# One more unit of seven products, squares on ScalarE and a new work order in a fused attention and FFN kernel

## The chip, the cores and the metric

The kernel runs on one core of one Trainium2 chip. The metric is the device time of one execution in microseconds (us). The time before is the median of three runs, 202.79 us (202.77 to 202.88).

## The reference

All tensors are bf16; there are 2048 tokens and a width of 640, 32 heads of 20, and an FFN width of 1728.

```python
xn = layernorm(x)                                  # per token, no weights
q, k, v = heads(xn @ wqkv)                         # wqkv: 640 x 1920
pq, pk = phi(q), phi(k)                            # phi(t) = (t + 1 if t > 0 else exp(t)) + 1e-6
kv = sum over tokens of pk^T v; z = sum of pk      # linear attention, no mask
s = ((pq @ kv) / (pq . z + 1e-6)) @ wo
g = silu(relu(xn @ w1) @ w2)                       # w1: 640 x 1728, w2: 1728 x 640
return x + s * g
```

## The kernel before

Tokens are cut into 16 tiles of 128, and four tiles make a chunk of 512. The width of 640 gives five pieces of 128 for the contraction.

**Stages.** In the head, tiles 0 to 3 are centred with a quick mean (`mean_act`, `centre`), transposed on TensorE (`transposes`), copied out of PSUM (`xcT_copy`) and multiplied with the key weights (`K_mm`); the missing scale 1/sigma is applied later, for keys in `K_exp` and `K_relu`, for FFN blocks in `scale_h`. Tiles 4 to 15 get their statistics (`bn` twice and `aggr`, or `LN_stats`), are normalised (`LN_norm`) and transposed by a DMA that `LN_norm` issues on SP's queue (`xnT_dma`, L703); tiles 0 to 3 get that normalised and transposed copy later too. The keys, query blocks (`Q_block`, 128 columns of q for one chunk) and FFN blocks (`H_block`, 128 columns of h for one chunk) follow, then the token sum of pk and x (`g` units, `G_last`), the denominators, the matrix that joins kv with wo, the second FFN product (`u` units) and the output product (`o` units).

**Units of seven.** Many products are done in pairs by a scheme of seven half-size products for eight (`unit`, `seven`): sums of weights (`h_S`, `q_S`, `m_S`, `k_S`) and sums of activations (`h_T`) are made on VectorE, each unit runs the steps s1, s5, s6, s2, s7, s3, s4 on TensorE over three PSUM banks, with evacuations on ScalarE and adds on VectorE between them. Units `a` and `p` are FFN and query blocks for chunks 0 and 1 (`jp` = 0), `b` and `q` those for chunks 2 and 3, `k` key tiles. Query block 4 and FFN block 12 have no partner of their own kind; for chunks 2 and 3 they form a unit together (`m_unit`, `m1`), for chunks 0 and 1 they are four plain blocks of five 512-column matmuls: block 12 of chunk 0 in the head (`HP`), `H112`, `Q04` and `Q14`.

**Order.** Each operation is recorded with what it reads and writes; `place` then plays the records through a table of estimated costs. TensorE and SP keep the order in which operations were recorded; ScalarE, VectorE and GpSimd do so up to `end_of_head`, and behind it may take any of the next 60 operations that is ready. The order of recording is written out by hand: the head as Python calls, everything behind it as words of `PROGRAM`, a few of which are `a0.s1` (step s1 of unit a0), `H14` (FFN block 4 of chunk 1), `n8` (statistics and norm of tile 8), `Ka8` (half of key tile 8), `y7` (pk of tile 7 added to the sum by a GpSimd DMA), `l0` and `l1` (the two pieces of the last output tile, cut at column `LC[1]`).

**The head's order on TensorE:** 32 small matmuls on constants, key products and transposes of tiles 0 to 3 as their loads come, FFN blocks 4, 5, 10, 11, 12 of chunk 0 (L804), key tiles 4 to 7 (L714), FFN blocks 10, 12, 4, 11, 5 of chunk 1, `Q14` (L766), then unit `a0` (L1203). **On SP's queue:** x 0, key weights in four loads, w1 pieces, x 4 to 7, w1 pieces, the transposes of tiles 4, 5, 6, 7, x 8-9, query weights, the transposes of tiles 0 to 3. x 1 to 3 are loaded from ScalarE's queue.

Of the kernel before, what the change touches and what calls it, by code (L numbers as in the profile page):

```python
# [95 lines left out]
class Sched:  # L96
# [44 lines left out]
    def _record(self, E, kind, fns, R, W, extra, sem=None):  # L141
# [5 lines left out]
        if kind == "dma":  # L147
# [12 lines left out]
            o.byt = 0.6 if o.turn else size / {"scr": 205e3}.get(names[0], {"scr": 240e3}.get(names[1], 310e3))  # L160
            lag = 0.5 if names[1] == "scr" else 0.8 if names[1] == "reg3" and names[0] == "reg6" else 0.0
            if o.turn and names[0] == "wv_sb":
                o.byt = 2.0
# [25 lines left out]
    def place(self):  # L189
# [16 lines left out]
        line = 2.0  # L206
        narrow = turned = False
# [4 lines left out]
        while left:  # L212
# [133 lines left out]
H110 H112 H14 H111 T0 H15 SQ SK xa Q14 a0.s1 a0.s5 Q04 a0.s6 p1.s5 p1.s1 n8 wa xb a0.s2 a0.s7 p1.s6 rb a0.s3 a0.s4 p1.s3 a1.s5 a1.s1 wb p1.s7 p1.s2 a1.s6 xc n9 SH1 p1.s4 a1.s2 Kb8 a1.s7 n12 n11 p0.s1 n10 n13 a1.s3 p0.s5 Ka8 p0.s6 n14 a1.s4 n15 y7 p0.s2 a2.s5 a2.s1 p0.s7 Ka12 a2.s6 Kb12 p0.s3 a2.s2 p0.s4 y8 a2.s3 a2.s7 hh0 hh1 T1 a2.s4 b0.s1 b0.s5 Ka11 b0.s6 k1.s1 k1.s5 b0.s2 k1.s6 b0.s7 b0.s3 k1.s7 k1.s2 b0.s4 k1.s3 k1.s4 Kb15 q0.s1 q0.s5 b1.s1 q0.s6 b1.s5 q0.s2 b1.s6 q0.s7 y6 q0.s3 b1.s3 q0.s4 mv6 b1.s7 b1.s2 y2 k2.s5 k2.s1 b1.s4 a3.s5 y3 k2.s6 Kb11 y9 a3.s1 k2.s2 k2.s7 k2.s3 a3.s6 k2.s4 a3.s2 a3.s7 a3.s3 q1.s1 q1.s5 a3.s4 q1.s6 b2.s5 q1.s2 SM y12 b2.s1 y13 Ka15 y0 q1.s7 w2a b2.s6 y4 y1 y14 GT1 GT2 y5 y15 q1.s3 y11 q1.s4 b2.s7 zm b2.s3 GS0 GT3 b2.s2 b3.s1 b2.s4 b3.s5 SH2 y10 b3.s6 m1.s5 m1.s1 b3.s2 b3.s7 m1.s6 b3.s3 m1.s2 b3.s4 m1.s7 zs b4.s5 GT4 m1.s3 b4.s1 m1.s4 c1 b4.s6 b5.s5 b5.s1 w2d c0 b4.s7 b4.s2 b4.s3 b5.s6 b4.s4 g0.s5 w2b g0.s1 b5.s7 b5.s3 b5.s2 zc g0.s6 b5.s4 dn g0.s3 g1.s1 GS1 g1.s5 g1.s6 g0.s7 g0.s2 w2c g1.s7 g1.s3 wv0 ZS uT3 wo do0 g1.s2 g1.s4 g0.s4 wv1 sl rc0 uSa0 uSb0 uT2 uT1 do3 do1 u0.s1 u0.s5 kv1 u0.s6 rc1 kv0 W5 u0.s7 u0.s2 W4 uT4 uSa2 dv1 u0.s3 W2 u0.s4 W1 W3 W0 xre dv0 uSa1 u1.s1 oT uSb2 uSb1 u1.s5 u2.s1 u2.s5 u1.s6 u2.s6 u2.s2 uSa4 u2.s7 oS0 u1.s7 u1.s3 u2.s3 u1.s2 u2.s4 u1.s4 do2 o0.s5 o0.s1 u4.s5 o0.s6 u4.s1 o0.s2 o0.s3 uSb4 o0.s7 u4.s6 o0.s4 u4.s2 o1.s1 oS2 uSa6 u4.s7 oS1 o1.s5 o1.s2 o1.s6 uSa3 u4.s3 o1.s3 o1.s7 u4.s4 o1.s4 u3.s5 o2.s1 u3.s1 rc3 o2.s5 o2.s2 o2.s6 u3.s6 uSb3 o2.s7 dv3 o2.s3 uSa5 u3.s7 o2.s4 u3.s2 o3.s1 rc2 u3.s3 u3.s4 oS3 uSb6 dv2 o3.s2 o3.s5 oS4 o3.s6 u5.s1 u5.s5 o3.s7 o3.s3 uSb5 u5.s6 u5.s2 o3.s4 u5.s7 u5.s3 o4.s1 u5.s4 o4.s5 o4.s2 o4.s6 u6.s1 u6.s5 oS5 u6.s6 o4.s3 o4.s7 u6.s7 o4.s4 u6.s3 oS6 o6.s1 o6.s5 u6.s2 o6.s6 u6.s4 o6.s2 o6.s7 o6.s3 e3 uSa7 o6.s4 u7.s1 o5.s5 o5.s1 u7.s5 o5.s6 u7.s6 o5.s7 o5.s2 o5.s3 u7.s2 o5.s4 e0 f0 uSb7 u7.s7 u7.s3 f3 e1 u7.s4 f1 l0 l1  # L346
# [3 lines left out]
def bass_recurrent_scan__linear_attn_block__dense_activation_relu__prompt_kernel(  # L350
# [300 lines left out]
    def LN_norm(t):  # L653
        norms.append(sc.op("DVE", lambda eng: eng.tensor_scalar(
            out=xn[:, t, :], in0=xin[:, xs(t), :], scalar1=mv[:, t, 0:1], scalar2=rsy[:, t:t + 1],
            op0=ALU.subtract, op1=ALU.mult), R=[("xin", xs(t)), ("mv", t), ("rsy", t)], W=[("xn", t)]))
# [175 lines left out]

    bn(0, 0)
    mean_act(0, HN)
    half_mean_dve(0)
    centre(0)
    mean_act(1, 0)
    transposes(0, 0)  # L840
    xcT_copy(0, 0, 0, "DVE")
    centre(1)
    fill(3)
    K_mm(0, 2, 0, 1)
    transposes(1, 6)
    xcT_copy(0, 0, 1, "DVE")
    mean_act(2, 0)
    xcT_copy(1, 6, 0, "DVE")
    xcT_copy(1, 6, 1, "ACT")
    K_mm(0, 2, 1, KA)  # L850
    K_mm(1, 4, 0, KA)
    centre(2)
# [12 lines left out]
    K_mm(2, 6, 0, KA)
    K_mm(2, 6, 2, 3)
# [1094 lines left out]
```

## Time and profile before

| | before |
|---|---|
| median of runs | 202.79 us |
| span of the profiled execution | 201.4 us |
| median less span | 1.4 us |
| TensorE busy | 197.8 us, 1340 matmuls |
| VectorE busy | 175.1 us |
| ScalarE busy | 130.9 us |
| GpSimd busy | 37.9 us |
| granted TensorE clock | 1.000 |

The profile gives the span from the first to the last instruction of one execution; what lies around it is seen only as the difference to the runs' median. Busy shares are means over stages: TensorE is the bound for most of the span and the others lie beside it. In the chain of waits each piece begins with the start time, then its length, then the engine and the line; "x25" is a count of instructions. A line of the groups ends with busy time, the mean of one in ns, and the idle time ahead of it.

### The profile page before, as it was taken

The page shows a single profiled execution, that of the slowest core. Times are in us where ns is not written, and L with a number is a line of the kernel's source. Part 1 is how long each engine was busy: PE and PEld are TensorE (multiplying, and loading weights), DVE is VectorE, ACT ScalarE, POOL GpSimd, SP SyncE. Part 2 cuts the span into 40 slices and gives each one's busy share as a digit, 9 for nine tenths or more (in the row PEclk, how much of TensorE's full clock was granted, in tenths as well). Part 3 has the DMA queues.
Part 4 walks back from the last instruction along what each step waited for, and adds up shares of the span by engine and source line. Part 5 has one row for each costly group of instructions (what it writes and reads, how often), then busy time and mean ns, then how long its engine had stood idle before and what let it go on. Part 6 is the DMA issues. An engine that isn't in the chain of part 4 may idle for free.

```text
span 201.4 us, 3693 instructions
## 1 busy us (share of the span) xinstructions
PE 197.8 (98%) x1340; PEld 122.6 (61%) x1340; DVE 175.1 (87%) x413; ACT 130.9 (65%) x273; POOL 37.9 (19%) x66
## 2 busy tenths in 40 slices
PE   8999999999999999999999999999999999999995
PEld 7655644455455454445654777777777777767773
DVE  5988999999999888999975999999779786985674
ACT  6598957998999999978653224371555555445643
POOL 3174060363134654152200000000000000000000
PEclk9999999999999999999999999999999999999999
DMA  6977974765545896575910987865961244012103
GB/s 196 326 211 120 264 174 30 189 164 119 116 92 107 163 260 131 102 142 104 245 34 2 324 217 207 263 201 145 373 232 65 68 163 165 0 67 68 65 33 98
DMA packets 38471, 30.43 MB, mean 151 GB/s; under 512 B 13749, under 2 KB 38453, under 8 KB 38453
## 3 DMA queue, kind: packets, MB, share of 16 engines
q1 hardware_dynamic: 32581, 23.28, 41.2%
q0 software_dynamic: 4624, 5.57, 14.3%
q10 hardware_dynamic: 1248, 1.35, 2.1%
q8 instruction: 10, 0.16, 0.3%
q14 instruction: 8, 0.07, 0.1%
HBM read 15.81 MB, written 5.24 MB: 105 GB/s over the span
## 4 chain that ended last, share of the span: by engine, by line
PE 95%; DMA 3%; SPq 1%; DVE 0%; issue 0%; DVEq 0%
PE psT L1030 43%; PE psT L1203 31%; PE psT L714 8%; PE psT L804 5%; DMA reg<-in_A_wqkv_dram 3%; PE psT L1501 2%; PE psT L1835 1%; PE psT L822 1%; PE psT L766 1%; PE psT L1626 1%; PE psT L1600 1%; PE psT L934 1%; DVE reg L975 0%; SPq L564 0%; SPq L540 0%
## 5 line engine op out<-in xcount | busy, mean ns | idle before, releaser
L1203 PE MATMUL psT<-reg 128*128 128x512 bf16 (+2 forms) x159 | 41.7, 370 | 0.0
L1030 PE MATMUL psT<-reg,regH 128*128 128x320 bf16 (+1 forms) x224 | 34.8, 299 | 0.0
L1030 PE MATMUL psT<-reg 128*128 128x320 bf16 (+1 forms) x178 | 29.4, 299 | 0.0
L1030 PEld LDWEIGHTS psT<-reg,regH 128*128 128x128 bf16 (+1 forms) x224 | 21.8, 98 | 8.7 <-DVE psT L975 0.2
L1203 PEld LDWEIGHTS psT<-reg 128*128 128x128 bf16 (+1 forms) x159 | 15.5, 98 | 16.1 <-DVE reg L975 0.7
L902 POOL DMA_DIRECT2D regH<-reg x16 | 18.4, 1238 | 27.0 <-DMA regH<-reg 9.4
L1037 ACT ACTIVATE reg<-psT 128x320 f32<-128x320 f32 (+1 forms) x24 | 10.4, 435 | 17.4 <-PE psT L1030 15.9
L1030 PEld LDWEIGHTS psT<-reg 128*128 128x128 f16 (+1 forms) x178 | 17.3, 98 | 7.2 <-DVE regH L1256 0.4
L975 DVE TENSOR_TENSOR reg<-reg 128x1024 f16<-128x1024 bf16 (+10 forms) x30 | 18.9, 645 | 0.7 <-PE psT L1203 0.6
L1253 ACT ACTIVATE regH<-psT 128x512 bf16<-128x512 f32 (+1 forms) x24 | 14.6, 607 | 4.1 <-PE psT L1203 3.9
L975 DVE TENSOR_TENSOR psT<-psT,reg 128x320 f32<-128x320 f32 (+1 forms) x22 | 11.9, 542 | 5.6 <-PE psT L1030 5.1
L1030 PE MATMUL psT<-reg,pqT 128*128 128x320 bf16 (+1 forms) x84 | 16.3, 299 | 0.0
L1662 ACT ACTIVATE wv_sb<-psT 128x320 bf16<-128x320 f32 (+1 forms) x22 | 9.2, 423 | 10.3 <-PE psT L1030 9.9
L635 DVE BATCH_NORM_STATS2 stats<-reg 128x6 f32<-128x320 bf16 x32 | 13.9, 475 | 1.9 <-DMA reg<-in_A_x_dram 1.9
L1850 ACT ACTIVATE reg<-psT 128x640 bf16<-128x640 f32 (+1 forms) x14 | 8.0, 570 | 9.2 <-PE psT L1030 9.2
L714 PE MATMUL psT<-reg 128*128 128x320 bf16 x80 | 12.3, 299 | 0.0
L1037 ACT ACTIVATE psT<-psT 128x320 f32<-128x320 f32 x17 | 7.3, 427 | 6.8 <-PE psT L1030 6.8
L975 DVE TENSOR_TENSOR reg<-psT,reg 128x320 f32<-128x320 f32 (+2 forms) x19 | 9.5, 504 | 1.4 <-PE psT L1030 1.3
L781 ACT ACTIVATE regE<-psT 128x512 bf16<-128x512 f32 x16 | 9.6, 607 | 1.1 <-PE psT L766 0.5
L714 PEld LDWEIGHTS psT<-reg 128*128 128x128 bf16 x80 | 7.8, 98 | 4.3 <-ACT regH L808 0.3
L643 POOL TENSOR_TENSOR rsy<-rsv,mhalf 128x1 f32<-128x1 f32 x16 | 10.0, 622 | 1.3
L1030 PEld LDWEIGHTS psT<-reg,pqT 128*128 128x128 bf16 (+1 forms) x84 | 8.2, 98 | 3.2
(170 smaller groups left out, 397.9 us busy)
## 6 DMA issues: line engine op xcount, KB each, us to landing
regH<-reg POOLq DMA_DIRECT2D x16, 320.0 KB, 3.7
reg<-in_B_w_dram SPq DMA_DIRECT2D x12, 320.0 KB, 4.6
scr<-rden SPq DMA_DIRECT2D x4, 640.0 KB, 6.7
reg<-in_A_x_dram SPq DMA_DIRECT2D x4, 640.0 KB, 6.3
out_dram<-reg SPq DMA_DIRECT2D x14, 160.0 KB, 1.8
regE<-scr SPq DMA_DIRECT2D x3, 640.0 KB, 5.3
reg<-in_A_x_dram SPq DMA_DIRECT2D x4, 320.0 KB, 3.8
reg<-in_A_wo_dram SPq DMA_DIRECT2D x6, 160.0 KB, 5.0
```

The source lines that it names most:

```text
L635: sc.op("DVE", lambda eng: eng.bn_stats(stats[:, t, a, :], xv[:, HN * a:HN * (a + 1)]), R=[("xin", xs(t))], W=[("stats", t, a)])
L643: sc.op("POOL", lambda eng: eng.tensor_tensor(out=rsy[:, t:t + 1], in0=rsv[:, t:t + 1], in1=mhalf[:, :], op=ALU.pow), R=[("rsv", t), ("mha ...
L714: fns.append(lambda eng, a=a, k=k, lhs=lhs: eng.matmul(ps[bk[a]][:, 0:HN], lhsT=lhs, rhs=wk[:, k, HN * a:HN * (a + 1)], start=(k == 0), st ...
L781: exps.append(sc.op("ACT", lambda eng: eng.activation(out=e_, in_=src, func=ACTF.Exp), R=[key], W=[("er_e", es)]))
L804: sc.group("PE", [(lambda eng, k=k: eng.matmul(ps[b], lhsT=w1_col(k, P * f, P), rhs=src[:, k, :], start=(k == 0), stop=(k == C - 1))) for ...
L902: dma("POOL", lambda eng: eng.dma_start(zacc[a], src, **kw), R=[key] + after, W=[("zacc", a)], chain=zchain[a])
L975: sc.op("DVE", lambda eng: eng.tensor_tensor(out=out, in0=in0, in1=in1, op=op), R=R, W=W, extra=extra)
L1030: sc.group("PE", [(lambda eng, k=k, lhs=lhs, rhs=rhs: eng.matmul(ps[b][:, 0:HN], lhsT=lhs, rhs=rhs, start=(start and k == 0), stop=(k == n ...
L1037: sc.op("ACT", lambda eng: eng.activation(out=dst, in_=ps[b][:, 0:HN], func=ACTF.Copy), R=[("ps", b)], W=[dkey], extra=extra)
L1203: sc.group("PE", [(lambda eng, k=k, lhs=lhs, rhs=rhs: eng.matmul(ps[b][:, 0:nn], lhsT=lhs if tile is None else rhs, rhs=rhs if tile is Non ...
L1253: sc.op("ACT", lambda eng: eng.activation(out=dst, in_=ps[b], func=ACTF.Relu), R=[("ps", b)], W=[("hT", j, f)], extra=ex)
L1662: sc.op("ACT", lambda eng, lo=lo, hi=hi: eng.activation(out=g[:, lo:hi], in_=src[:, lo - HN * n:hi - HN * n], func=ACTF.Silu), R=[key, ("s ...
```

## The change

1. FFN block 12 and query block 4 of chunks 0 and 1 become a unit `m0` by the existing `m_unit`; block 12 leaves `HP` (the blocks of chunk 0 made from unscaled tiles). `m_unit` writes chunk 0's FFN half as f16.
2. For tiles 1 and 2 the variance comes from ScalarE: `square` squares the centred tile with an accumulated output, and `root` gives the inverse root on GpSimd. Their `bn` and `aggr` go; `LN_norm` takes the mean from `msum`.
3. The head is written as words of `PROGRAM` too (up to the word `|`), and all words have a new order. Tile 0's norm and DMA transpose (`N0`) come right after the third group of TensorE transposes; the order of DMA transposes is 0, 6, 4, 5, 7, 2, 3, 1 and then tile 8. x 2 and x 3 are loaded by SP, key weights in pieces 0-1, 2-3 and 4; the last w1 piece (`lw6`) is loaded behind the head.
4. The last output tile is cut at 192 instead of 160, and the planner's DMA costs are changed.

```diff
-            o.byt = 0.6 if o.turn else size / {"scr": 205e3}.get(names[0], {"scr": 240e3}.get(names[1], 310e3))
+            o.byt = 0.6 if o.turn else size / {"scr": 205e3}.get(names[0], {"scr": 240e3, "in_A_x_dram": 365e3, "in_A_wqkv_dram": 365e3}.get(names[1], 300e3))
...
+        lags = [(3.8, 0.6), (13.0, 0.7)]
...
-                line = max(est + (2.0 if c.turn else 1.5), line + (0.8 if turned and not c.turn else 0.0)) + c.byt
+                line = max(est + (2.0 if c.turn else 1.5), line + (turned != c.turn) * (0.4 if c.turn else 0.8)) + c.byt
+                if lags and line > lags[0][0]:
+                    line += lags.pop(0)[1]
...
-H110 H112 H14 H111 T0 H15 SQ SK xa Q14 a0.s1 a0.s5 Q04 a0.s6 p1.s5 p1.s1 n8 wa xb a0.s2 ...
+lx0 ax1 ma0 ba0 ma1 mh0 ce0 lx2 lk02 bb0 ce1 lx3 lk24 ag0 lk45 lx6 tr0 ma2 ca0 lx4 sq1 lw2 ma3 pf3
+lw0 ce2 cd1 lx5 sq2 tr1 cd2 lw5 lx7 k001 ba3 k012 lw3 tr2 N0 k102 ca5 cd3 mh3 ce3 S6 S4 k024 ca4
+N6 S5 N4 k123 k134 bb3 k145 ag3 tr3 N5 k045 S7 SH0_1 ca6 lx8 ca7 k204 k245 N7 ke0 kr0 lq ke2 N2
+N3 ke1 SH0_3 kr1 kr2 |
+SQ N1 F0 k304 P5 S8 k345 wb lw6 xb n8 xa P4 SM ke3 n12 F1 P11 mv6 rb wa xc kr3 P10
+F3 KT4 SK KT5 F2 KT6 KT7 n9 SH1 n10 SH0_2 n11 n14 n15 F7 H14 n13 F6 y0 H110 y7 H15 y3 a0.s1
+p1.s1 y1 T0 y2 p1.s5 a0.s5 H111 a0.s6 p1.s6 SH0_4 F4 F5 p1.s2 a0.s2 a0.s7 p1.s7 Ka8 a0.s4 Kb8 a0.s3 y4 p1.s4 m0.s1 p1.s3
+y8 m0.s5 a1.s1 m0.s6 m0.s2 Ka12 a1.s5 a1.s6 Kb12 m0.s7 m0.s3 a1.s7 m0.s4 a1.s3 ...
...
+    def square(t):
+        junk = ek[:, eks(t), 1, :]
+        sc.op("ACT", lambda eng: eng.activation(out=junk, in_=xn[:, t, :], func=ACTF.Square, scale=D ** -0.5,
+                                                accum_out=mv[:, t, 1:2]), ...)
+        root(t)
...
     def LN_norm(t):
+        mean, key = (msum[:, t, 1:2], ("msum", t, 1)) if t in BY_ACT else (mv[:, t, 0:1], ("mv", t))
...
-                sc.op("ACT", lambda eng: eng.activation(out=hT[:, NF - 1, schunk(j)], in_=ps[b], func=ACTF.Relu),
+                sc.op("ACT", lambda eng: eng.activation(out=(hT if j else hTh)[:, NF - 1, schunk(j)], in_=ps[b],
...
-    HP = (4, 5, 10, 11, 12)
+    HP = (4, 5, 10, 11)
...
-    LC = [0, 160, 320]
+    LC = [0, 192, 320]
```

In the new words `lx`, `lk` and `lw` are loads of x, key weights and w1, `ma` a mean on ScalarE, `ba` and `bb` the two halves of the statistics, `ag` their aggregate, `sq` a square, `ce` a centring, `tr` a group of TensorE transposes, `cd` and `ca` copies of a transposed half tile on VectorE and ScalarE (the number is twice the tile, plus the half), `k024` key tile 0's pieces 2 and 3, `ke` and `kr` its exp and relu, `S` and `N` statistics and norm with DMA transpose, `P5` FFN block 5 of chunk 0, `KT4` a whole key tile, `F` the sum of a key tile's two parts.

More of the change, by code (lines that the diff above doesn't have):

```diff
@@ L347 @@
+o6.s5 o6.s6 o6.s2 u7.s7 f3 o6.s7 o6.s3 u7.s3 f1 e0 o6.s4 u7.s2 f0 u7.s4 l0 l1
 """
@@ L1928, in bass_recurrent_scan__linear_attn_block__dense_activation_relu__prompt_kernel @@
         "y": z_add,
+        "lx": x_load,
+        "ax": lambda t: x_load(t, 1, "ACT"),
+        "lw": lambda d: w1_load(d, d + 1, "SP"),
+        "ba": lambda t: bn(t, 0),
+        "bb": lambda t: bn(t, 1),
+        "mh": half_mean_dve,
+        "sq": square,
+        "ce": centre,
+        "tr": head_turn,
+        "cd": lambda n: head_copy(n, "DVE"),
+        "ca": lambda n: head_copy(n, "ACT"),
+        "pf": fill,
+        "ag": aggr,
+        "ke": head_exp,
+        "kr": head_relu,
+        "P": head_block,
+        "KT": K_tile,
+        "S": S, "N": N, "F": F,
     }
```

171 lines of the change are left out of this document (76 added, 95 removed).

## The prediction

> **What bounds the kernel now.** I read the page's busy times and the summary of its chain first, then who waited on TensorE, then the chain in order of time.
>
> ```profile
> PE 197.8 (98%) x1340; PEld 122.6 (61%) x1340; DVE 175.1 (87%) x413; ACT 130.9 (65%) x273; POOL 37.9 (19%) x66
> PE 95%; DMA 3%; SPq 1%; DVE 0%; issue 0%; DVEq 0%
> ```
> ```profile
> PE psT L603 <- PEq L1946: 0.8, 1, 0.8
> PE psT L714 <- DMA reg<-in_A_wqkv_dram: 0.3, 1, 0.3
> ```
> ```profile
> 2.19 5.20 DMA reg<-in_A_wqkv_dram
> ...
> 7.43 1.53 PE psT L714 x10
> 8.96 0.28 PE psT L687 x5
> 9.24 2.99 PE psT L714 x22
> 12.23 5.40 PE psT L804 x25
> 17.62 5.47 PE psT L714 x40
> 23.09 5.40 PE psT L804 x25
> 28.49 1.08 PE psT L766 x5
> 29.57 0.86 PE psT L1203 x4
> ...
> 198.33 0.36 PE psT L1835 x5
> ...
> 198.79 0.30 DVE reg L975
> ...
> 199.13 0.62 DVE reg L975 x3
> ```
>
> The waits say that TensorE stands still twice: 0.8 us before its first instruction and 0.3 us for a piece of the key weights, which lands at 2.19 + 5.20 = 7.39. From 7.43 to 198.69 each piece of the chain begins where the last one ended. So three things can move the end: how much TensorE has to do, how early its stream becomes gapless, and the 2.7 us behind its last matmul (201.4 - 198.7). The span is 201.4, the median of the runs 202.79; 1.4 us lie outside the span and I leave them as they are. A measurement of this kernel can tell about 0.2%, 0.4 us, from no change.
>
> The page "Perfetto Trace Analysis" of the Trainium skill, section "Identifying the Most-Contended Engine", says that matmul occupancy is a poor measure of how near TensorE is to its limit and that the share of weight loads is a better one. Here that share is 61%, by which two matmuls less would be worth nothing and the sum below would lose its first term; the gapless chain speaks for the 98%.
>
> **Part 1: the unit of seven.** Query block 4 and FFN block 12 for chunks 0 and 1 are four blocks of five 512-column matmuls now, 20. The unit has products of 2, 2, 2+1, 3, 3, 3 and 2 matmuls, 18. One costs 5.40 / 25 = 0.216 us (row at 12.23), so **-0.43 us** on the path. What the unit asks of the other engines:
>
> ```profile
> L1210 ACT ACTIVATE psT<-psT 128x512 f32<-128x512 f32 x15 | 9.2, 610 | 0.0
> L975 DVE TENSOR_TENSOR psT<-psT,wv_sb 128x512 f32<-128x512 f32 x10 | 6.9, 694 | 1.0 <-PE psT L1203 1.0
> L1266 DVE TENSOR_SCALAR regH<-regH 128x512 bf16<-128x512 bf16 x10 | 3.0, 322 | 0.1
> L975 DVE TENSOR_TENSOR regH<-regH,wv_sb 128x512 f16<-128x512 bf16 x5 | 1.8, 418 | 0.0
> L635 DVE BATCH_NORM_STATS2 stats<-reg 128x6 f32<-128x320 bf16 x32 | 13.9, 475 | 1.9 <-DMA reg<-in_A_x_dram 1.9
> L639 DVE BATCH_NORM_AGGREGATE mv<-stats 128x2 f32<-128x12 f32 x16 | 3.3, 204 | 0.3
> L666 ACT ACTIVATE regE<-reg 128x640 bf16<-128x640 bf16 x2 | 1.5, 728 | 0.0
> ```
> ```profile
> L666 ACT ACTIVATION_READ_ACCUMULATOR regE<-reg x4: 186/186/187, 3.7 to 6.8; 128x1 f32 x4
> ```
> ```profile
> 5.00:40.00 35.00, 34.71 (x206) 18.76 (x204) 32.96 (x93) 27.90 (x51) 11.57 (x29) 1.00 0.79 187
> 40.00:100.00 60.00, 60.00 (x347) 30.61 (x346) 57.61 (x139) 54.76 (x117) 24.79 (x28) 1.00 0.67 144
> ```
>
> ScalarE evacuates seven times instead of six (two copies, two exp and two relu, one FFN relu): +0.61. VectorE gets two f32 adds and a relu more (0.69 + 0.69 + 0.32) and one row scaling less (0.42), since block 12 of chunk 0 no longer reads unscaled tiles: +1.28. All of that can lie beside matmuls if it keeps pace.
>
> **Part 2: squares on ScalarE.** Tiles 1 and 2 lose four statistics and two aggregates on VectorE, 4 x 0.475 + 2 x 0.204 = 2.3, and gain two squares with their accumulator reads on ScalarE, 2 x (0.73 + 0.19) = 1.8. Together with part 1 VectorE has 1.0 us less and ScalarE 2.4 more. By the windows (columns: stretch, length, PE, weight loads, VectorE, ScalarE) VectorE has 2.0 us free between 5 and 40 and ScalarE 7.1, so the exchange fits where it is made. From 40 to 100 both are nearly full (57.6 and 54.8 of 60): cover is thin there, and if it is gone, what TensorE waits for is an add or an evacuation of about 0.6 us.
>
> **Part 3: the new head, up to 7.4 us.**
>
> ```profile
> 4.58 0.74 ACT L666 ACTIVATE regE<-reg 128x640 bf16<-128x640 bf16 x1
> 4.50 0.63 PE L687 MATMUL psT<-ident,reg 128*128 128x128 bf16 x5
> 5.03 0.38 DVE L676 TENSOR_SCALAR reg<-reg,msum 128x640 bf16<-128x640 bf16 x1
> 5.96 0.49 ACT L699 ACTIVATE regX<-psT 128x384 bf16<-128x384 bf16 x1 [0.55 <-PE psT L687]
> 6.70 0.44 PE L687 MATMUL psT<-ident,reg 128*128 128x128 bf16 x5
> ```
> ```profile
> L564 SPq DMA_DIRECT2D reg<-in_A_wqkv_dram x4: 417/432/439, 1.3 to 2.7; - x4
> ...
> DMA to landing us min/median/max: 2.9/4.4/5.7
> ```
>
> Tile 0's first copy goes to ScalarE behind the third mean: 4.58 + 0.74 + 0.1 for the accumulator's rest = 5.4, and a copy of at most 0.49, so the first key matmuls start near 5.8 instead of 5.2. Tile 1's centring stays near 5.1 (one statistic, 0.4, takes the place of a copy ahead of it), its transposes near 5.5. By 7.2 TensorE can have done the 8 key matmuls and 15 transposes that it has done now by 7.1 (last row at 6.70, 0.28 net by the chain) before it waits for weights. The next step (k024) needs weight pieces 2 and 3 in one load. On the queue that is the load with 8 tiles' worth of bytes through it (four x tiles, four weight pieces); now the third piece, 7 tiles' worth, lands at 7.39, and the last load, 9 worth, at 2.66 + 5.7 = 8.4. Between them is 7.9. So k024 starts between 7.2 (nothing waits: -0.25 against 7.43) and 7.9 (+0.45). I take neither end: the middle, 7.5, about **+0.1**.
>
> The page "DMA: Bandwidth & Descriptors" of the Trainium skill, section "Bandwidth", lists a 1 MB load at 341 GB/s; by that, as an estimate, eight tiles' worth (1.31 MB) takes 3.8 us, lands near 7 and the wait goes, which would make this term -0.25. The 7.39 of the row is slower than that, so I keep the middle. That x tiles 2 and 3 move from ScalarE's queue to SP's costs two issues of 0.43 (row L564) ahead of the weights, already in the 7.9.
>
> **Part 4: the transposed tiles.** Tile 0's DMA transpose now goes first, then tiles 6, 4, 5, 7, 2, 3, 1, with the load of x 8-9 after tile 5 and the query weights after tile 7.
>
> ```profile
> L703 SPq DMA_TRANSPOSE reg<-reg x4: 1200/1270/1497, 14.1 to 18.5; - x4
> ...
> DMA to landing us min/median/max: 2.6/2.7/3.3
> ```
> ```profile
> 13.68 0.39 DVE L654 TENSOR_SCALAR reg<-reg,mv,rsy 128x640 bf16<-128x640 bf16 x1
> 19.71 0.58 SPq L540 DMA_DIRECT2D reg<-in_A_x_dram  x1
> 20.34 0.47 SPq L545 DMA_DIRECT2D reg<-in_A_wqkv_dram  x1
> 20.86 5.90 SPq L703 DMA_TRANSPOSE reg<-reg  x4
> ```
> ```profile
> reg<-in_A_wqkv_dram SPq DMA_DIRECT2D x1, 800.0 KB, 5.3
> ```
>
> First gate, key tile 4. Now its norm runs at 13.68, its transpose is issued at 14.10 and lands at 17.4 (14.1 + 3.3), just ahead of its matmuls at 17.62. With block 12 gone (five matmuls, 1.08) those come at 16.54 if the head is even. Tile 0's transpose waits for tile 0's norm, and all others queue behind it on SP; that norm needs only tile 0's own statistics, which stand early in VectorE's order, so I cost the wait at nothing. Ahead of tile 4's norm VectorE does 3 statistics and 2 aggregates less and 2 norms more: -(1.4 + 0.4) + 0.8 = -1.0; but tile 5's x, whose statistics stand in front, comes one tile later. I put the norm at 13.0, 0.7 earlier, the transpose at 13.4, landing 16.1 to 16.7 (2.7 to 3.3). That is even, to within 0.3.
>
> Second gate, tile 1, the last of chunks 0 and 1, which the first step of a unit needs. An even head brings TensorE there at 16.54 + 5.47 + 3 x 1.08 = 25.25. On the queue after tile 4's 13.4: two transposes and x 8-9 by 16.7, tile 7 by 18.0, query weights at 18.1, three transposes of 1.48 (5.90 / 4) end at 23.0, plus 1.4 from the end of an issue to landing (2.7 - 1.27): 24.5. But the weights need 5.3 from issue, 23.4, and now the last of four transposes lands 2.6 behind them (26.76 + 1.4 against 25.6), so three land 2.0 behind: 25.4. So 24.5 to 25.4 against 25.25. The VectorE sums that the next products need (0.68 each) start at that landing, behind two products of 0.43, so they fit. I take **-0.1** for parts 3 and 4 beyond the +0.1: the middle, 25.0, is 0.25 ahead of the need, and can be used only as far as the stream ran ahead. Head together **0.0**, from -0.25 to +0.45.
>
> Behind these stand the remaining tiles: key halves of tile 8 now come about 6.3 us after that step, near 31.5; its queue (one 320 KB and one 240 KB weight load, 320 KB of x after tile 1) at the 187 GB/s of the first window takes 4.8 us, so about 30.5 with its own transpose. One microsecond of cover.
>
> **Part 5: the tail.** The last tile's two pieces become 192 and 128 columns. The first multiplication starts 32 columns of five matmuls later, 0.36 / 5 = 0.07, and lasts 0.30 x 32 / 160 = 0.06 longer; the second and the adds get shorter by some 0.08. **+0.05**.
>
> **Sum:** 202.79 - 0.43 + 0.0 + 0.05 = **202.4**.
>
> **Rivals.**
> (a) *The loads come before TensorE wants them.* Weights by 7.2, tile 1 by 25.0: -0.25 more, 202.15. The floor lies lower: from 4.50 to 7.43 TensorE has real work for 15 x 0.056 + 8 x 0.137 = 1.9 (0.28 / 5 and 5.47 / 40), so the head can give 1.0 at the very most, 201.4; half of that, with the tail, is 201.9. For it: no load in the trace is late by more than 0.3. Against: bytes ahead of the weights grow.
> (b) *The gates hold the head.* Weights at 7.9 and tile 1 at 25.4 or later: +0.4, 202.8, no change.
> (c) *Slower: tile 4's transpose takes the place of block 12.* Two transposes, tiles 0 and 6, of 1.27 issue each stand in front of it, and TensorE gets there 1.08 sooner. If it lands when it does now, 17.4, the matmuls start at 17.5 rather than 16.54: +1.0, 203.4. It decides once the landing passes 16.8, where the -0.38 is used up. For it: 3.3, the longest landing, is that of the first transpose behind the loads. Against: VectorE's 1.0 us less.
> (d) *Slower: new waits between 30 and 100.* Every unit moved; one add or evacuation of 0.6 late on a full VectorE or ScalarE costs up to 0.6, two of them 203.2.
> (e) *The unit saves nothing*, because TensorE is not the bound: 202.8. The chain is against it.
>
> **How the numbers follow.** Forecast 0.42 (its own range 202.1 to 202.7), (a) 0.20, (b) 0.12, (c) 0.12, (d) 0.12, (e) 0.02. Faster by over 0.4 us (below 202.38): half of the forecast and all of (a) and a little of (d), 0.46. Slower (above 203.2): (c) and most of (d), with what of (b) goes further, 0.25. Same: 0.29. The range takes in (a) to its 201.9, rounded down, and (c): 201.8 to 203.4.
>
> **What would show it.** TensorE's work from its first gapless step to its end shorter by 0.43 (18 matmuls for 20); k024 between 7.2 and 7.9; key tile 4 near 16.5 and the first unit step near 25.2, with no wait or one under 0.3 naming a DMA; from there no TensorE wait. Wrong would be a TensorE wait of over 0.5 on a transposed tile, any wait behind 30 us, or a chain that leaves TensorE for VectorE.

## The result, and the profile after

The changed kernel takes 204.31 us (median of 4 runs, 203.86 to 204.39), the kernel before on the same chip 202.78 (202.29 to 202.88): a ratio of 1.0074, interval 1.0059 to 1.009. It is slower by 1.5 us and lies above the range of the prediction. The profiled execution took 204.39 with a span of 203.10, against 201.41 before.

The page's busy times and its summary of the chain, after:

```profile
PE 198.0 (97%) x1328; PEld 122.8 (60%) x1338; DVE 172.8 (85%) x407; ACT 131.9 (65%) x280; POOL 36.7 (18%) x66
PE 65%; DVE 20%; DMA 5%; ACT 3%; SPq 2%; issue 2%; POOL 1%; DVEq 0%
```

The chain of before was TensorE for 95%; now a third of it lies elsewhere, most of that on VectorE and on DMAs. (Ten matmul records are missing on the first line: 1338 weight loads, 1328 matmuls. Missing ones show as gaps of exactly one matmul and are not counted as idle here.) Who waited on TensorE, after:

```profile
PE psT L604 <- PEq L1966: 0.8, 1, 0.8
PE psT L1163 <- DMA reg<-reg: 0.7, 1, 0.7
PE psT L732 <- DMA reg<-reg: 0.7, 1, 0.7
```

The wait for key weights is not there, and two new ones name `reg<-reg`, a DMA that moves SBUF to SBUF: the transposes. Their places in TensorE's timeline (start, length, engine, line, then the count; the last bracket is the idle time and its releaser):

```profile
15.70 1.03 PE L822 MATMUL psT<-regX,reg 128*128 128x512 bf16 x4
17.39 1.79 PE L732 MATMUL psT<-reg 128*128 128x320 bf16 x12 [0.66 <-DMA reg<-reg]
...
24.76 1.46 PE L822 MATMUL psT<-reg 128*128 128x512 bf16 x6
26.95 1.04 PE L1163 MATMUL psT<-reg 128*128 128x512 bf16 x4 [0.73 <-DMA reg<-reg]
```

Back to back, four matmuls of 0.216 from 15.70 end the FFN blocks at 16.56, and key tile 4 starts at 17.39: **gate 1, 0.83 us**. Six from 24.76 end at 26.06, and the first unit step starts at 26.95: **gate 2, 0.89 us**. The same places in the kernel before:

```profile
14.66 2.97 PE L804 MATMUL psT<-regX,reg 128*128 128x512 bf16 x13
17.50 1.79 PE L714 MATMUL psT<-reg 128*128 128x320 bf16 x12
```
```profile
28.33 1.24 PE L766 MATMUL psT<-reg 128*128 128x512 bf16 x5
29.41 0.59 PE L1203 MATMUL psT<-reg 128*128 128x512 bf16 x2
```

There 13 matmuls from 14.66 end at 17.46 and key tile 4 follows 0.04 later; the first unit step follows without a wait at 29.41. Without block 12 (1.08) the blocks would have ended at 16.38, so the changed head is 0.2 behind before it comes to gate 1. These three, 0.2 + 0.83 + 0.89 = 1.9 us, small waits behind 30 us of about 0.3 (the largest 0.23 at 67.3), 0.43 off for the unit and 0.12 off for the tail come to 1.65 of the 1.69 us by which the span is longer.

When the transposes landed is in the view of their line on SP's queue; first the four issued from 9 to 16.1 us (tiles 0, 6, 4, 5), then the four from 17 (7, 2, 3, 1); the last line of each is the time from issue to landing:

```profile
L721 SPq DMA_TRANSPOSE reg<-reg x4: 1199/1563/2144, 9.2 to 14.2; - x4
...
DMA to landing us min/median/max: 3.5/4.7/6.9
...
L721 SPq DMA_TRANSPOSE reg<-reg x4: 1214/1250/2379, 17.1 to 21.6; - x4
...
DMA to landing us min/median/max: 3.3/5.2/5.8
```

Before, the first four took 2.6 to 3.3. Single landings from the trace: tile 0 issued 9.16, landed 16.05; tile 6 16.53; tile 4 issued 12.99, landed 17.26; query weights issued 18.37, landed 24.20; then tile 2 24.85, tile 3 25.44, tile 1 (issued 21.59) 26.91.

### The profile page after: what moved, and what is told of

Read it like the earlier page. It is cut to its first block, busy times and chain, and to the rows that moved or that the text cites. A ratio compares the mean times of both kernels' runs of the same rounds, so it can differ in the third digit from the quotient of the medians.

```text
span 203.1 us, 3686 instructions
## 1 busy us (share of the span) xinstructions
PE 198.0 (97%) x1328; PEld 122.8 (60%) x1338; DVE 172.8 (85%) x407; ACT 131.9 (65%) x280; POOL 36.7 (18%) x66
## 4 chain that ended last, share of the span: by engine, by line
PE 65%; DVE 20%; DMA 5%; ACT 3%; SPq 2%; issue 2%; POOL 1%; DVEq 0%
PE psT L990 42%; PE psT L1163 17%; DMA reg<-in_A_x_dram 3%; DVE psT L935 3%; DVE stats L636 3%; DVE regH L935 2%; DMA reg<-reg 2%; PE psT L1493 2%; DVE reg L935 2%; DVE reg L672 2%; DVE reg L760 2%; DVE pqT L935 2%; ACT regE L742 1%; PE psT L1837 1%; SPq L561 1%
## 5 line engine op out<-in xcount | busy, mean ns | idle before, releaser
L1163 PE MATMUL psT<-reg 128*128 128x512 bf16 (+2 forms) x159 | 42.2, 370 | 1.1 <-DMA reg<-reg 0.7
L990 PE MATMUL psT<-reg 128*128 128x320 bf16 (+1 forms) x178 | 28.7, 299 | 0.0
L1163 PEld LDWEIGHTS psT<-reg 128*128 128x128 bf16 (+1 forms) x166 | 15.7, 98 | 18.9 <-DMA reg<-reg 1.2
L935 DVE TENSOR_TENSOR reg<-reg 128x1024 f16<-128x1024 bf16 (+11 forms) x30 | 19.1, 650 | 1.6 <-PE psT L990 0.7
L1664 ACT ACTIVATE wv_sb<-psT 128x320 bf16<-128x320 f32 (+2 forms) x22 | 9.2, 425 | 8.2 <-PE psT L990 7.9
L636 DVE BATCH_NORM_STATS2 stats<-reg 128x6 f32<-128x320 bf16 x28 | 12.5, 480 | 2.3 <-DMA reg<-in_A_x_dram 2.2
L732 PE MATMUL psT<-reg 128*128 128x320 bf16 x80 | 12.3, 299 | 0.7 <-DMA reg<-reg 0.7
L1170 ACT ACTIVATE psT<-psT 128x512 f32<-128x512 f32 (+1 forms) x18 | 10.6, 596 | 0.8 <-PE psT L1163 0.7
L732 PEld LDWEIGHTS psT<-reg 128*128 128x128 bf16 x80 | 7.8, 98 | 5.2 <-ACT regH L826 1.1
```

Source lines behind the costliest of these rows:

```text
L636: sc.op("DVE", lambda eng: eng.bn_stats(stats[:, t, a, :], xv[:, HN * a:HN * (a + 1)]), R=[("xin", xs(t))], W=[("stats", t, a)])
L732: fns.append(lambda eng, a=a, k=k, lhs=lhs: eng.matmul(ps[bk[a]][:, 0:HN], lhsT=lhs, rhs=wk[:, k, HN * a:HN * (a + 1)], start=(k == 0), st ...
L935: sc.op("DVE", lambda eng: eng.tensor_tensor(out=out, in0=in0, in1=in1, op=op), R=R, W=W, extra=extra)
L990: sc.group("PE", [(lambda eng, k=k, lhs=lhs, rhs=rhs: eng.matmul(ps[b][:, 0:HN], lhsT=lhs, rhs=rhs, start=(start and k == 0), stop=(k == n ...
L1163: sc.group("PE", [(lambda eng, k=k, lhs=lhs, rhs=rhs: eng.matmul(ps[b][:, 0:nn], lhsT=lhs if tile is None else rhs, rhs=rhs if tile is Non ...
L1170: sc.op("ACT", lambda eng: eng.activation(out=dst[:, 0:nn], in_=ps[b][:, 0:nn], func=ACTF.Copy), R=[("ps", b)], W=[dkey], extra=extra)
```

## Experiments

Theory A, formed from this: the transposes land at times that loads and SP's queue set, not TensorE; the plain blocks 12 and query 4 were the work that covered those times, and with four blocks less in the stretch up to the first units (block 12 of chunks 0 and 1, `Q14`, and `H111`, which moved behind the first unit steps; 4 x 1.08 = 4.3 us), TensorE runs into two gates, one behind the other. Rival B: the two waits are separate and add up. Rival C (the waits only show a loss that lies elsewhere) and later D, F, G, H stand with the runs. The expectations of e1 to e4 use other letters: theory G there is A, rival U is B. All ratios are to the kernel before on the same chip, with their intervals; the changed kernel stands at 1.0074 (1.0059 to 1.009).

| run | median us | ratio (interval) |
|---|---|---|
| e1_t4_first | 209.36 | 1.0324 (1.0288 to 1.036) |
| e2_h111_first | 206.22 | 1.0198 (1.0146 to 1.025) |
| e3_x8_late | 207.35 | 1.0257 (1.0223 to 1.029) |
| e4_t4_first_x8_late | 209.53 | 1.0362 (1.0309 to 1.0415) |
| g1_kt4 | 204.20 | 1.0083 (1.0047 to 1.0119) |
| g2_t1 | 203.58 | 1.0054 (1.003 to 1.0077) |
| g12 | 203.34 | 1.0044 (1.002 to 1.0068) |
| u1_unit_alone | 208.99 | 1.0302 (1.0257 to 1.0347) |
| f1_fetch | 203.99 | 1.0063 (1.0045 to 1.0082) |
| f2_fetch2 | 203.95 | 1.0063 (1.0043 to 1.0084) |
| f3_kt6_first | 203.66 | 1.0047 (1.0033 to 1.0061) |
| f4_split_weights | 204.41 | 1.01 (1.0076 to 1.0125) |
| c1_plain | 205.69 | 1.0153 (1.0135 to 1.0171) |
| s1_squares | 204.79 | 1.0102 (1.0087 to 1.0118) |
| s2_squares_fixed | 202.84 | 1.0007 (0.9996 to 1.0017) |
| t1_tail | 202.50 | 0.9998 (0.9989 to 1.0006) |

### Words moved in the order (e1 to e4)

```diff
 e1:  -tr2 N0 k102 ... -N6 S5 N4 ... tr3 N5 k045      +tr3 N5 N0 N6 k045
 e2:  -p1.s5 a0.s5 H111 a0.s6    +H15 y3 H111 a0.s1
 e3:  -ca6 lx8 ca7               +SQ N1 lx8 F0
 e4:  e1 and e3 together
```

> The norms and DMA transposes of tiles 0 and 6 move behind tile 5's, nothing else. Theory G (two gates in series: TensorE loses 0.82 us at the key matmuls of tile 4, which start at 17.4, and 0.90 at the first unit step, which starts at 26.95 when tile 1 lands; the later gate sets the time): tile 4 lands near 16.1, its matmuls start at 16.6, and the wait at the first unit step grows from 0.9 to about 1.7 because tile 1 lands no earlier; time as the changed kernel's, 204.3 +- 0.3. Rival U (each gate costs on its own): 203.5. Rival L (tile 4 is held by the loads ahead of all transposes, not by tiles 0 and 6): its matmuls still start at 17.4 and nothing changes.

> FFN block 11 of chunk 1 (five matmuls, 1.08 us) moves from behind four unit steps to ahead of the first. Theory G: it covers the 0.90 at the second gate, unit a0 starts at 27.2 without a wait, time about 203.5; with some of it given back at a0.s6, which needs the third VectorE sum, 203.8. Rival: the VectorE sums of activations, not the landing, hold the units: the wait moves to a0.s6 in full and the time stays at 204.3.

> The load of x 8-9 moves on SP's queue from ahead of tile 7's transpose to behind tile 1's. Theory G: tile 7, the query weights and tiles 2, 3, 1 come 1 to 2 us earlier, tile 1 lands by 25.5, the first unit step starts near 26.1 without a wait, the tile 4 wait stays: about 203.4. If tile 8 then comes too late for its key half, part of this is lost there. Rival (tile 1 is held by the issue of transposes on SP or by a slow DMA engine, not by the bytes ahead): tile 1 still lands at 26.5 to 26.9, no gain.

> Both of the moves: tiles 0 and 6 behind tile 5, and x 8-9 behind tile 1. Theory G: both waits go (0.82 and 0.90), about 202.6, as far as tile 1 lands by 25.3. Rival U for the first and no gain for the second: 203.5. Nothing gained: 204.3.

All four are far slower than expected. TensorE's waits of e1, then of e3:

```profile
PE psT L1163 <- DMA reg<-reg: 2.4, 1, 2.4
PE psT L705 <- DVE reg L698: 1.0, 1, 1.0
...
PE psT L732 <- DMA reg<-reg: 0.5, 1, 0.5
```
```profile
PE psT L732 <- DMA reg<-reg: 2.4, 2, 1.7
PE psT L881 <- DVE regE L935: 1.5, 1, 1.5
```

In e1 tile 4's transpose goes first and lands at 16.19, 2.70 behind its issue, and key tile 4 does not wait; but TensorE comes there only at 18.53 in this execution, so that the old landing would have done as well. Tiles 0 and 6 now stand behind it, the unit's first step comes at 30.37, and the wait there (L1163) grows from 0.7 to 2.4. The matmuls behind that wait run at half speed until 33.5 us (last section), which is part of e1's price. In e3 the load of x 8-9 is out of the way, tile 1 lands at 25.79 and gate 2 is gone; key tile 8 pays instead (L732, 1.7 near 34), and a product at 104 waits 1.5 for VectorE. In e2 the block H111 covers gate 2, and waits of 0.2 to 0.7 for ScalarE and VectorE come up later. So the gates move as A has it, but the prices do not fit. A moved word also makes the planner choose another order behind the head: the traces of e1, e2 and e3 show other orders on VectorE and ScalarE. That this makes up the rest of the price is likely and not shown here; s1 and s2 show it for another edit. From here on, in all g and f runs and s2, ScalarE, VectorE and GpSimd keep the order of the kernel they start from, by a list; in u1, c1 and s1 they do not.

### The gates taken away (g1, g2, g12)

```diff
 g1:   K_mm of tile 4
-      xnT[:, t // 4, k, P * (t % 4):P * (t % 4 + 1)]
+      xnT[:, 0, k, 0:P]                                  # tile 0's
 g2:
+      memset(xnT[:, 0, :, P:2 * P], 0.25)                # at the start, VectorE
       tile 1's dma_start_transpose
-      to xnT[:, 0, :, P:2 * P]
+      to pk[:, 15, :]
 g12:  both
```

> The changed kernel, every engine's order as it was, but key tile 4 multiplies tile 0's transposed copy (landed at 16.05) instead of tile 4's (17.26): the first gate is taken away, the computation of that one tile is wrong. Theory A, two gates in series: tile 1's transpose lands when it lands (26.9), whatever TensorE did before; the 0.82 us won at key tile 4 is lost again at a0.s1, whose wait grows from 0.9 to about 1.7; 204.3 us, as the changed kernel. Rival B, the two waits are independent and add up: 0.8 us less, 203.5. Rival C, the time is lost elsewhere and the waits only show it: 204.3 with the wait at a0.s1 unchanged at 0.9.

> The changed kernel, every engine's order as it was, but tile 1's DMA transpose writes to an unused place and its columns of the transposed copy are filled with a constant at the start (its part of the products is wrong): the second gate is taken away, the queue keeps its eight transposes. Theory A: a0.s1 starts at 26.1 instead of 26.95, since tile 3's transpose has landed at 25.4; 0.85 us less, 203.4 to 203.5. The wait at key tile 4 stays 0.8. Rival B (independent waits) says the same here, rival C: no gain, 204.3.

> Both gates taken away together. Theory A: a0.s1 is wanted at 25.2 and now has tile 3's transpose (25.4) and the activation sums on VectorE behind it; between 1.2 and 1.6 us less than the changed kernel, 202.7 to 203.1. That is more than the sum of the two single steps (0 and 0.85), which is what tells A from B: B gives 0.8 + 0.85 = 1.7 from two steps of 0.8 and 0.85. Rival C: 204.3.

TensorE's waits of g1, g2 and g12 in turn (the 0.8 of the first instruction left out):

```profile
PE psT L1170 <- DMA reg<-reg: 1.0, 1, 1.0
...
PE psT L739 <- DMA reg<-in_A_wqkv_dram: 0.6, 1, 0.6
```
```profile
PE psT L744 <- DMA reg<-in_A_wqkv_dram: 0.6, 1, 0.6
```
```profile
PE psT L744 <- DMA reg<-in_A_wqkv_dram: 0.4, 1, 0.4
PE psT L713 <- DVE reg L706: 0.3, 1, 0.3
PE psT L744 <- DMA reg<-reg: 0.3, 1, 0.3
```

g1 tells A from B: without gate 1 the time stays (204.20), and a0.s1 still starts at 26.95. Its wait there grows only from 0.9 to 1.1 and not to 1.7, because this execution had already waited 0.6 for the weights of pieces 2 and 3 (the line with L739). Removing a gate that has a later one behind it gains nothing. Against the changed kernel's ratio g2 gained 0.4 us and g12 0.6, half of what A expected, and the intervals overlap, that of g12 by a little (1.0059 to 1.0068); the waits at a0.s1 are gone in both traces (that of g2 is of an execution 1.1 us above its median, last section). What took the rest stands in the waits: the first key products (L744) wait for the first load of key weights, and in g12 key tile 5 waits 0.3 for its own transpose, landed at 18.08. The profiled execution of g12 (203.04, the fastest of its ten) did gain what A expected: its span is 201.74, 1.36 less than that of the changed kernel.

By the medians alone rival C would stay open. The traces of the runs with one and the same order settle it. Start of a0.s1, of a0.s6 (the first unit step behind H111) and of the last matmul:

| run | a0.s1 | a0.s6 | last matmul | from a0.s6 to the last |
|---|---|---|---|---|
| changed kernel | 26.95 | 29.77 | 200.55 | 170.78 |
| g1_kt4 | 26.95 | 29.77 | 200.55 | 170.78 |
| f1_fetch | 26.64 | 29.46 | 200.24 | 170.78 |
| f2_fetch2 | 26.67 | 29.47 | 200.26 | 170.79 |
| f3_kt6_first | 25.71 | 29.14 | 199.92 | 170.78 |
| g12 | 25.52 | 28.58 | 199.19 | 170.61 |

From a0.s6 on the stream takes the same time, to 0.2 us, however late it begins, and in the first five to 0.01. Nothing that is lost before it is made up later, and nothing more is lost: with this order, what decides is when TensorE gets through the second gate.

### The unit alone, and everything but the unit (u1, c1)

```diff
 u1, on the kernel before:
-    HP = (4, 5, 10, 11, 12)
+    HP = (4, 5, 10, 11)
-    H110 H112 H14 H111 T0 H15 SQ SK xa Q14 a0.s1 a0.s5 Q04 a0.s6
+    H110 H14 H111 T0 H15 SQ SK xa a0.s1 a0.s5 a0.s6
     ... m0.s1 to m0.s4 between p1.s4 and p0.s6, SM ahead of them
     key tiles 4 to 7 in other PSUM banks
 c1, on the changed kernel:
-    m0.s1 ... m0.s5 ... m0.s6 m0.s2 ... m0.s7 m0.s3 ... m0.s4
+    Q04 ... Q14 ... H012 ... H112                       # plain, at the same place; SM later
```

> The kernel before with part 1 alone: block 12 leaves the head, Q14, Q04 and H112 go, the unit m0 stands beside a1, with the weight sums it needs; no squares, old head, old order of loads and transposes. Theory A, the plain blocks were the cover of the transposes: key tile 4 comes at 16.54 and waits for its transpose (landed at 17.37) 0.85 us, a0.s1 comes at 27.2 and waits for tile 3's (28.19) 1.0 us; -0.43 + 1.85 = +1.4, 204.2, about as the whole change. Rival D, the new order is to blame and the unit itself does what the count of matmuls says: 202.4.

> The changed kernel with the unit alone undone: query block 4 and FFN block 12 of chunks 0 and 1 are four plain blocks again, near 36 to 42 us where the unit was, and its weight sums move to where the kernel before had them; squares, head, order of loads and transposes, both gates stay. Theory A: the unit's own term is two matmuls, and four plain blocks this late cover no gate: 0.43 us more, 204.7. Rival H, the unit's evacuations and sums on the full VectorE and ScalarE cost what the matmuls save, and the small waits behind 30 us are its own: 204.3 or less.

TensorE's waits of u1:

```profile
PE psT L1203 <- DMA reg<-reg: 1.2, 1, 1.2
PE psT L1203 <- DVE regE L975: 1.1, 1, 1.1
PE psT L1203 <- ACT pqT L783: 0.9, 1, 0.9
```

Both expectations of u1 are wrong by size. A's mechanism is on the first two lines: the first unit step waits 1.2 for tile 3's transpose, which lands at 27.86 (28.19 before), and the next product 1.1 for the sums that VectorE makes of it. The plain blocks had covered that second step too, which no theory had counted. The rest of the 5.0 us that its span is longer are new waits from 38 us on (the third line and smaller ones) in an order that was planned anew. Rival D's 202.4 does not hold: the wait for the transpose alone, 1.2, is more than the 0.43 that the unit saves. How much of the whole is the unit's and how much the planner's u1 cannot tell.

c1 is 1.4 us slower than the changed kernel by the median, on the other side from rival H. But ScalarE, VectorE and GpSimd were planned anew here too, and that alone costs more than this in s1 below, so c1 does not price the unit. Its profile shows where the excess over 0.43 is:

```profile
PE psT L732 <- DMA reg<-reg: 0.6, 1, 0.6
PE psT L1631 <- ACT wv_sb L1667: 0.5, 1, 0.5
```

The second wait stands at 131 us, far behind the edit; the first is gate 1, unchanged. In that execution tile 1 landed at 25.32 and gate 2 was open: a0.s6 starts at 28.96, 0.81 earlier than in the changed kernel, and from there to the last matmul it takes 172.39, 1.6 more. So what c1 lost it lost behind 30 us, 0.43 of it for the two matmuls.

### What sets gate 2, and whether gates add up (f1 to f4)

In the changed kernel 15 of the 16 parts of tile 1's transpose land by 26.00, and one at 26.91, behind an instruction fetch of 8 KB that starts at 25.38 (both by the trace's single packets and landings). The DMA view from 25 to 27.2 us has the fetch:

```profile
q14 instruction: 1, 0.01, 0.9%
```

```diff
 f1:  "lw6" (second load behind tile 1's transpose)    + waits for the transpose to land
 f2:  "wb"  (first load behind it)                     + waits for the transpose to land
 f3:  f2 and  -F3 KT4 SK KT5 F2 KT6 KT7    +F3 F2 KT6 KT4 SK KT5 KT7
 f4:  f3 and  -ce0 lx2 lk02 bb0            +ce0 lk01 lx2 lk12 bb0
```

> The changed kernel, every engine's order as it was, but the load of the last w1 piece waits for tile 1's transpose to land. In the changed kernel 15 of 16 parts of that transpose land by 26.00 and the last at 26.91, 1.5 us after an 8 KB instruction fetch that began at 25.38, 0.2 us after the third load behind the transpose was issued; in g1_kt4, g2_t1 and g12 the same load, fetch and late part follow each other. Theory F, the fetch holds one part of the transpose up: with the three loads held until the landing the fetch comes behind it, the transpose lands at 26.0, a0.s1 starts at 26.1 instead of 26.95, and the time is 203.4 to 203.5. Rival G, the last part is late for another reason (the transpose's own issue, the loads behind it): it lands at 26.9 still, 204.3. If the later loads cost more than they give: a wait on tile 8's key half near 33, and over 204.3.

> The changed kernel, every engine's order as it was, but the first load behind tile 1's transpose (w1 piece 4) waits until that transpose has landed, and the other loads stand behind it. In f1_fetch, where only the second load waited, the fetch still came 1.37 us after the first one was issued, as in the changed kernel (1.42) and g12 (1.36), and the last part of the transpose was 0.95 us late again. Theory F, the fetch holds one part up: now it comes behind the landing, all parts land within 0.2 us of each other near 25.6 to 26.0, a0.s1 waits under 0.1, 203.4 to 203.6. Rival G, the last part of the last transpose is late whatever follows: landing spread over 0.9 again, 204.0 to 204.3. A third possibility: the fetch comes at the same time although nothing is issued; then it isn't moved by this and F and G stay untold.

> As f2_fetch2, and key tile 6, whose transpose lands at 16.5, is multiplied ahead of key tile 4 (17.3), so that the first gate is gone without any work left out. Theory A (gates in series): TensorE reaches a0.s1 0.8 us sooner and waits there for tile 1's transpose near 25.6 to 26.0 instead; little or nothing against f2_fetch2, 203.3 to 203.6. Rival B (waits add up): 0.8 less than f2_fetch2, 202.6 to 202.8, level with the kernel before.

> As f3_kt6_first, and the first load of key weights is split again: piece 0 in front of x 2, piece 1 behind it. In nine of twelve profiles with the changed head the first key products wait 0.4 to 1.2 us for the load of pieces 0 and 1 (it lands at 5.0 to 6.8; piece 0 alone lands at 4.0 to 5.2 in the old head). Theory A (gates in series): the head comes 0.5 to 1.0 sooner and waits at the tiles' transposes instead, which land when they land: 203.4 to 203.7, as f3_kt6_first. Rival B (waits add up): 202.8 to 203.1.

f1 did not move the fetch (it came at 25.03, 1.37 behind the issue of the first load again), and the last part was 0.95 late again. In f2 nothing was issued, the fetch still came at 25.30, in front of the landing, and the parts landed within 0.27 us of each other. That is the third case of its expectation, so f2 by itself does not tell F from G. Over all profiles with this head: of the ten with a load issued behind tile 1's transpose, seven (the changed kernel, g1, g2, g12, e2, e4, f1) have a fetch of 0.33 us and one part 0.87 to 0.95 late; of the three without (f2, f3, f4) none has one that is over 0.2 late. A late part was seen only with a load behind, which speaks for G as the expectation of f1 has it (the loads behind it). It is not the whole of it: c1, e1 and e3 have the load and no such part, and in c1, e3 and f3 the fetch itself took 0.7 to 0.84 us. Why one or the other goes first stays open. The time of f2 did not fall below f1's. Its waits on transposes and weights, then those of f3:

```profile
PE psT L741 <- DMA reg<-in_A_wqkv_dram: 1.1, 1, 1.1
...
PE psT L741 <- DMA reg<-reg: 0.6, 1, 0.6
```
```profile
PE psT L741 <- DMA reg<-in_A_wqkv_dram: 0.8, 1, 0.8
PE psT L1172 <- DVE regE L944: 0.4, 1, 0.4
```

f3 takes gate 1 away with the whole computation kept: TensorE reaches the first unit step at 25.71, and there the next one stands: tile 1's transpose lands at 25.55, VectorE's sum of it is ready at 27.13, and the second product waits (0.4 on the last line). By the table above a0.s1 starts 0.96 earlier than in f2 and a0.s6 only 0.33; the medians gained 0.3 us (the intervals overlap) where B wanted 0.8. With g1 that is twice the same answer: the waits stand in series, and what is won at one is lost at the next, down to what the latest chain (query weights, tiles 2, 3, 1, sum) leaves.

f4 was to take the wait for the first weights away and missed both expectations. ScalarE's timeline of f4 shows why the first key products did not come earlier:

```profile
5.57 0.74 ACT L691 ACTIVATE regE<-reg 128x640 bf16<-128x640 bf16 x1 [1.00 <-DMA reg<-in_A_x_dram]
...
6.31 0.36 ACT L724 ACTIVATE regX<-psT 128x256 bf16<-128x256 bf16 x1
```

The split put x 2 one place back; the mean of tile 2 (L691) now waits 1.0 us for it, and the first copy of tile 0's transposed half (L724), which the first key products need, is queued behind that mean: 6.31 where f3 has it at 5.14. The first key products start at 6.72 in f4 and at 6.66 in f3, so the split gained nothing. The profiled execution took 205.48, 1.1 over its median, for a reason that is told in the last section; why the median itself, 204.41, is above f3's is open. (The expectation's "nine of twelve" was a miscount: in six of the twelve the first key products wait for that load, 0.3 to 1.1 us.)

### The small parts alone (s1, s2, t1)

```diff
 s1, on the kernel before:  bn, aggr of tiles 1 and 2 in the head  ->  square(1), square(2); LN_norm by msum
 s2:  s1 with the order behind the head held as in the kernel before
 t1:  -    LC = [0, 160, 320]
      +    LC = [0, 192, 320]
```

> The kernel before with part 2 alone: squares with accumulated output on ScalarE for tiles 1 and 2 in the head, their bn and aggregates gone. The prediction's part 2 (the exchange is free): 202.5, the same. Rival: two more operations of 0.9 us on ScalarE push the copies or the key evacuations behind them, a TensorE wait up to 0.6 in the head: 203.1.

> As s1_squares, but behind the head ScalarE, VectorE and GpSimd keep the order that they have in the kernel before (in s1_squares the planner had made a new one, and its waits stood at 29, 35, 54 and 59 us, none in the head). If the exchange itself is free, as part 2 had it: 202.6 to 202.8, the same as the kernel before. If the squares cost by themselves: above 203.5.

> The kernel before with the cut of the last output tile at 192 alone. The prediction's part 5: +0.05. By the two traces (2.72 us behind the last matmul before, 2.59 after): -0.12, 202.65; the only part of the change that I can still expect to gain anything by itself.

TensorE's waits of s1, and the only one of s2:

```profile
PE psT L839 <- DMA reg<-reg: 0.6, 1, 0.6
PE psT L1216 <- DVE regH L988: 0.5, 1, 0.5
```
```profile
PE psT L610 <- PEq L1966: 0.8, 1, 0.8
```

The squares are free to within 0.35 us (s2: ratio 1.0007, interval 0.9996 to 1.0017). s1, the same operations, costs 2.1 us, all of it by the order that the planner made of it behind the head. The cut of the last tile is worth nothing that can be measured; +0.05 and -0.12 both lie inside t1's interval. No version beat the kernel before.

## Why the prediction was wrong, point by point

- **The unit, -0.43: right.** TensorE's stream from 7.08 to 200.51, less 2.0 us of waits and four key matmuls (0.55) that the other trace had done by then, is 190.9 us; before it is 198.69 - 7.43 = 191.3, so it got shorter by about 0.4. The rule that was weighed there, from the page "Perfetto Trace Analysis" of the Trainium skill, section "Identifying the Most-Contended Engine" (the share of weight loads as the better measure, 61% here), would have given zero as the prediction read it.
- **Part 2, free: right** to within 0.35 us (s2, in the old head), on the condition that the rest keeps its order.
- **Part 3, +0.1: near in this profile, by another cause.** The weights of pieces 2 and 3 landed at 7.40, ahead of the 7.9 by the row, and nothing waited for them; k024 starts at 7.62, behind four key products at half speed (last section). The estimate by the page "DMA: Bandwidth & Descriptors" of the Trainium skill, section "Bandwidth", had been 7, which is 0.4 early here. Over the profiles with this head these weights land at 7.0 to 8.1, and in g1, at 8.05, they cost 0.6. What the step had left out is the load before it: pieces 0 and 1 in one load land at 5.0 to 6.8, and in six of twelve profiles the first key products wait 0.3 to 1.1 us for it. In the changed kernel the gates behind it would swallow that; it shows once they are removed.
- **Part 4, -0.1: the step that failed, at both gates.** At the first, the norm of tile 4 came earlier than predicted (12.56, not 13.0) and the transpose later: issued 12.99, landed 17.26, 4.3 us behind its issue where 2.7 to 3.3 was taken from the old rows. Those rows were of transposes that went out when all loads but one had landed, tile 4's ahead of the others. Here two others stand in front of it, nothing moves from 14.4 to 15.7 (last section), and then they land in order, 16.05, 16.53 and 17.26. In e1 and e4, where tile 4's goes out first, at 13.49 and 13.25, it lands 2.7 behind its issue. So the step priced a transpose by its own issue, where the landing is set by what is ahead of it in the queue.
- **The second gate, 24.5 to 25.4 against 25.25: wrong by 1.5, and this is the term that set the time.** The weights landed at 24.20 where 23.4 was taken, 0.8 of it. The transposes end 1.8 to 2.0 behind them in c1, e3, f2, f3 and f4, near the 2.0 that was taken, and 2.7 with the late part, the other 0.7. So tile 1 landed at 26.91. Rival (b) had this gate, but at +0.4.
- **"Head together 0.0": it was +1.9**, 0.2 for the slow start, 0.83 and 0.89 at the gates. The two gates were priced one by one, and as g1 and f3 show, only the last one counts: TensorE's place behind gate 2 is the landing of tile 1, 26.91, whenever it came there. Rival (c) had gate 1 right, 0.83 for its 1.0, and its reason in part (two transposes stand in front of tile 4's); with gate 2 where it was, it changed nothing by itself. All three signs that were named as wrong are there: waits of over 0.5 on transposed tiles, waits behind 30 us, and a chain that leaves TensorE for VectorE.
- **Rival (d):** waits behind 30 us are there, 0.3 rather than 0.6. The microsecond of cover for tile 8 held: no wait on it.
- **Part 5, +0.05:** nothing measurable (t1). The trace has 203.10 - 200.51 = 2.59 us behind the last matmul, before 2.72.

## What to carry to other kernels

Work that looks dear because it has no partner may be the cover of a transfer: before it is taken out, list the landings that it hides, and price only the last of them, since waits behind one another are lost and won together. A DMA that goes out behind loads lands in the queue's time, not its own: add its spacing to the landing of what is ahead. And where a planner orders the other engines, an experiment compares nothing until that order is held fixed: the same squares cost 2.1 us or nothing.

## What the runs showed of the hardware

**The transposes stood still during an instruction fetch.** The DMA view from 13.9 to 15.1 us has one fetch of 16 KB; from the trace it lasts from 13.93 to 15.02. Its line, then the busy share and the GB/s of the view from 13 to 17 us, in 40 slices of 0.1 us:

```profile
q8 instruction: 1, 0.02, 5.6%
```
```profile
DMA  9962620099999990000010000002999999999999
GB/s 192 123 59 64 41 28 18 18 233 418 274 274 271 253 18 0 0 0 0 0 8 8 10 10 8 10 10 59 252 290 292 287 289 220 270 282 287 292 294 246
```

Data starts to move again at 13.8, when the last load is about to land (13.96) and tile 0's transpose is next; it stops at 14.4 and goes on at 15.7, 0.7 us behind the fetch's end. In the eleven profiles with this head in which transposes were queued by then, the next one lands 0.9 to 1.2 us behind that end. In e1 and e4, where the first transpose went out only at 13.49 and 13.25, it lands 2.7 behind its issue. That the fetch is what stops them is not shown, only that the two go together. Without the standstill of 1.3 us tile 4 would have landed near 16.0, ahead of its need at 16.56, and gate 1 would be gone; that is an estimate from these rows, since no run moved this fetch.

**TensorE runs at half speed at first, for a time that differs from run to run.** Key matmuls of the same stretch in f3 and in f4:

```profile
7.48 2.06 PE L741 MATMUL psT<-reg,regX 128*128 128x320 bf16 x14
```
```profile
8.30 2.98 PE L741 MATMUL psT<-reg,regX 128*128 128x320 bf16 x14
```

The 14 of f3 begin 136 ns apart. The first seven of f4 begin 267 ns apart, half the speed, and the others 136. The windows view shows a granted clock of 1.00 there all the same; in f4's trace the record of the clock begins only at 10.15, with the short ones. The change comes between 3.4 and 6.7 us in 14 of 18 profiles and near 10 us in four (e1, e2, g2, f4). In these four TensorE stood waiting for 0.6 to 1.2 us near 5 or 6 us while it was still slow; f2 and f3, fast since 5.3 and 4.0, waited as long there and stayed fast. The profiled executions of e2, g2 and f4 are 1.1 to 1.8 us above the medians of their runs, so their waits and spans are not those of a typical run. In f4 the slow stretch costs most of 1.7 us by 17 us. In the changed kernel's profile it lasts to 6.7 and is the 0.2 us of the head. The page "TensorE: Matmul & The Clock Gate" of the Trainium skill, section "Part 1: The HAM clock gate", has this: half clock until one busy window of about 3.4 us, with a phase that varies from run to run. The trace agrees with the factor and the variation; its remark that only the first 3.4 us are slow does not hold in four of these profiles.

**In e1 it fell back to half speed behind a long wait.** The window from 30 to 33.5 us of e1 (length; then busy time and count of TensorE, weight loads, VectorE, ScalarE and GpSimd; granted clock, DMA share, GB/s):

```profile
30.00:33.50 3.50, 3.13 (x8) 1.16 (x9) 3.15 (x7) 1.52 (x3) 0.00 (x0) 0.51 1.21 271
```

TensorE had waited 2.4 us there, and its matmuls then begin 0.43 us apart instead of 0.216 until 33.5. Three of e1's four runs have a mean granted clock of 0.992, which is what one such stretch makes of 208 us, and the fourth, at 1.000, is 1.3 to 1.5 us faster. By an estimate from these rows, 2.4 us and half of 3.4, the wait cost e1 about 4. Single runs of e4, g1, g2 and g12 and two of u1 have 0.992 too; the waits in them were not profiled.
